# Quadrant matmuls, column-tiled kv and longer DMA runs in a fused attention and MoE kernel

## The chip, the cores and the metric

One core of one Trainium2 chip. The metric is device time in microseconds (us) from the first to the last instruction's completion, as the runs report it; lower is better. A profiled execution also has a span, which is about 1.7 us shorter than the reported time of the same run. The TensorE clock that was granted is given as a share of full speed.

## The reference, cut to what matters

```python
# q, k, v: (8 batches, 8 heads, 576 tokens, 64); w_in (512, 2048), w_out (2048, 512), beta (2048)
q_s = softmax(q, axis=-1)                       # over the 64 features of a head
k_s = softmax(k, axis=2)                        # over the 576 tokens
kv  = einsum('bhsd,bhse->bhde', k_s, v)         # 64 x 64 per head
x   = einsum('bhsd,bhde->bhse', q_s, kv)        # -> (4608 tokens, 512)
h   = x @ w_in
g   = h * sigmoid(beta * h)
out = g @ w_out
```

All inputs and outputs are float32; the kernel multiplies in bfloat16.

## The kernel before

The kernel works on nine chunks of 512 tokens: the first 512 tokens of each batch, and one chunk that holds the last 64 tokens of all eight batches. A chunk has 16 units. A unit is four h matmuls (512 columns each), a tanh on ScalarE and a multiply on VectorE that makes g. Four acc matmuls (g times w_out, 512 columns) of an older chunk are put between two units. The attention of the next batch is slipped in between: exponentials, sums, the kv matmuls (k_s times v) and the x matmuls (q_s times kv).

Two heads share the 128 rows. So kv of a pair of heads is a 128x128 product of which only two 64x64 blocks are wanted, and x uses a block-diagonal matrix `kvp` whose other half is zeros:

```python
    def kv_mm(b, j, n="K"):
        ...
        for t in range(K5):                       # 5 token groups
            nc.tensor.matmul(
                kvs[b, j // 2][:, j % 2, :],                                    # 128 x 130
                Ek[b][:, t, 2 * j : 2 * j + 2, :].rearrange("p h d -> p (h d)"),
                va[b % 2][:, t, j, :],
                start=(t == 0), stop=(t == K5 - 1),
            )

    def x_mm(b, j, n=None):
        ...
        nc.tensor.matmul(
            xps[b, j][:], kvp[b][:, j, :], qT[b][:, :, j, :], start=True, stop=True
        )
```

The loads of batches 0 and 1 and of w_in, and the way the first part is ordered:

```python
    def load_q(b, hf):                            # 1 KB runs, all 128 partitions
        ...
        nc.sync.dma_start(
            t,
            q[b, 4 * hf : 4 * hf + 4, 0:CH, :].rearrange("h (p t) d -> p h (t d)", t=NT),
        )
    ...
    load_w_in(0, 256, 0, 2)                       # 256-column blocks: 1 KB runs
    load_w_in(0, 256, 2, 4)
    for n0 in (256, 512, 768):
        load_w_in(n0, n0 + 256)
    ...
    dummy(24)                                     # matmuls on zeros while the loads come
    q_exp(0, 0, 4)
    q_exp(0, 4, 8)
    q_sum(0, 0, 4)
    q_div(0, 0, NT, nc.gpsimd, 0, 4)              # the two divisions on two engines
    q_sum(0, 4, 8)
    k_exp(0, 0, 4)
    q_div(0, 0, NT, nc.vector, 4, 8)
    ...
```

The softmax here doesn't subtract the row's maximum and nothing guards it: scores larger than these inputs give would overflow.

## Time and profile before

| | before |
|---|---|
| time, median of 3 runs | 287.14 us (286.96 to 287.19) |
| first h matmul starts | 14.40 us |
| first acc matmul (batch 0's h is done) | 30.09 us |
| last of batch 0's values v has landed | 12.98 us |
| last of batch 1's values v has landed | 46.05 us |
| span | 285.5 us |

From the page of the kernel before: the busy time of the engines, the TensorE row of the 40 slices (a digit is tenths busy), the shares of the chain that ended last, and two groups of instructions (line, engine, operation, shapes, count; busy us and mean ns of one; idle time before them and what ended it). PE is TensorE's matmuls, PEld its weight loads, DVE VectorE, ACT ScalarE, POOL GpSimd; SPq is the queue of SyncE, which issues most DMAs.

```profile
span 285.5 us, 4276 instructions
PE 279.2 (98%) x1490; PEld 133.3 (47%) x1490; DVE 157.8 (55%) x303; ACT 169.5 (59%) x275; POOL 79.4 (28%) x135
PE   8998999999999999999999999999999999999995
PE 82%; DMA 14%; POOL 1%; SPq 1%; issue 0%; ACT 0%; POOLq 0%; ACTq 0%
...
L415 PE MATMUL h<-xT,w_in_b 128*128 128x512 bf16 x512 | 129.6, 379 | 1.2 <-DVE g L429 0.6
L415 PEld LDWEIGHTS <-w_in_b 128*128 128x128 bf16 x576 | 56.1, 98 | 69.2 <-POOL w_in_b L154 2.9
```

TensorE is busy 98% and is 82% of the chain. A matmul's 379 ns is its whole passage; what counts for time is the distance between starts, and the timeline of TensorE shows it. Here is the steady state before (start, busy us of the group, what, count):

```profile
114.78 0.73 PE L283 MATMUL kv<-va,Ek 128*128 128x130 bf16 x10
115.35 1.03 PE L467 MATMUL acc<-w_out_b,g 128*128 128x512 bf16 x4
116.21 1.03 PE L415 MATMUL h<-xT,w_in_b 128*128 128x512 bf16 x4
117.07 0.38 PE L360 MATMUL x<-qT,kvp 128*128 128x512 bf16 x1
117.29 1.03 PE L467 MATMUL acc<-w_out_b,g 128*128 128x512 bf16 x4
```

Four acc take 116.21 - 115.35 = 0.86 us, so 216 ns each. Ten kv matmuls take 115.35 - 114.78 = 0.57 us, so 57 ns each, and a batch has 20: 1.14 us. One x takes 0.22 us, and a batch has four: 0.86 us.

The start is bound differently. These are the stretches view (from and to in us, length; busy time of PE, PEld, DVE, ACT and POOL, each with its count of instructions; granted TensorE clock; DMA share; GB/s) and, below it, the DMA view of the first 16 us in 40 slices of 0.4 us, before:

```profile
0.00:8.00 8.00, 6.75 (x18) 2.49 (x19) 3.41 (x10) 3.60 (x4) 5.81 (x23) 1.00 0.79 245
8.00:16.00 8.00, 7.73 (x80) 4.51 (x78) 5.96 (x16) 6.16 (x10) 5.01 (x9) 1.00 1.08 355
16.00:32.00 16.00, 14.86 (x68) 6.24 (x67) 10.92 (x16) 10.88 (x16) 12.05 (x16) 1.00 1.05 381
44.00:56.00 12.00, 11.71 (x75) 6.05 (x73) 9.98 (x24) 11.28 (x20) 4.66 (x6) 1.00 1.07 364
```
```profile
GB/s 0 0 0 0 18 74 205 369 381 369 384 376 356 313 312 338 369 313 349 374 350 378 353 364 374 359 352 360 356 366 349 351 348 341 341 353 356 346 351 351
```

DMA is full from 2.8 us on, at about 355 GB/s. TensorE's clock shows no half-speed stretch behind the dummies. The view counts time before the first clock record (7.20 us here) as 1.00. TensorE is idle for 1.1 us between 16 and 32 us.

### The profile page before, as it was taken

The page shows a single profiled execution, that of the slowest core. Times are in us where ns is not written, and L with a number is a line of the kernel's source. Part 1 is how long each engine was busy: PE and PEld are TensorE (multiplying, and loading weights), DVE is VectorE, ACT ScalarE, POOL GpSimd, SP SyncE. Part 2 cuts the span into 40 slices and gives each one's busy share as a digit, 9 for nine tenths or more (in the row PEclk, how much of TensorE's full clock was granted, in tenths as well). Part 3 has the DMA queues.
Part 4 walks back from the last instruction along what each step waited for, and adds up shares of the span by engine and source line. Part 5 has one row for each costly group of instructions (what it writes and reads, how often), then busy time and mean ns, then how long its engine had stood idle before and what let it go on. Part 6 is the DMA issues. An engine that isn't in the chain of part 4 may idle for free.

```text
span 285.5 us, 4276 instructions
## 1 busy us (share of the span) xinstructions
PE 279.2 (98%) x1490; PEld 133.3 (47%) x1490; DVE 157.8 (55%) x303; ACT 169.5 (59%) x275; POOL 79.4 (28%) x135
## 2 busy tenths in 40 slices
PE   8998999999999999999999999999999999999995
PEld 2543445454454444444454445444544444444444
DVE  3856347976866485647564766466553433334401
ACT  4776258957964587358845884568453544454411
POOL 7667954540631054104510261017000000000000
PEclk9999999999999999999999999999999999999999
DMA  7999999989499917990699059913300111031112
GB/s 232 356 365 386 381 354 353 363 211 363 102 217 360 179 38 174 356 226 36 135 322 282 20 129 238 350 39 78 110 37 0 73 39 38 0 75 39 37 73 74
DMA packets 55782, 51.67 MB, mean 181 GB/s; under 512 B 21184, under 2 KB 48208, under 8 KB 55760
## 3 DMA queue, kind: packets, MB, share of 16 engines
q1 hardware_dynamic: 55584, 51.33, 61.2%
q8 instruction: 11, 0.18, 0.3%
q14 instruction: 11, 0.09, 0.1%
q10 hardware_dynamic: 176, 0.07, 0.1%
HBM read 38.28 MB, written 9.44 MB: 167 GB/s over the span
## 4 chain that ended last, share of the span: by engine, by line
PE 82%; DMA 14%; POOL 1%; SPq 1%; issue 0%; ACT 0%; POOLq 0%; ACTq 0%
PE acc L467 39%; PE h L415 39%; DMA wo<-in_moe_w_out_dram 4%; DMA q<-in_q_dram 4%; PE kv L283 2%; DMA k<-in_k_dram 2%; DMA v<-in_v_dram 2%; DMA wi<-in_moe_w_in_dram 2%; PE x L360 2%; SPq L124 0%; PE xt L385 0%; POOL va L154 0%; SPq L122 0%; PE kv L310 0%; ACT xT L145 0%
## 5 line engine op out<-in xcount | busy, mean ns | idle before, releaser
L429 DVE SCALAR_TENSOR_TENSOR g<-th,h 128x512 bf16<-128x512 bf16 x144 | 98.3, 686 | 96.8 <-ACT th L427 96.6
L427 ACT ACTIVATE th<-h,beta_h 128x512 bf16<-128x512 f32 x144 | 98.4, 688 | 88.6 <-PE h L415 88.4
L467 PE MATMUL acc<-w_out_b,g 128*128 128x512 bf16 (+2 forms) x608 | 145.0, 368 | 0.0
L415 PE MATMUL h<-xT,w_in_b 128*128 128x512 bf16 x512 | 129.6, 379 | 1.2 <-DVE g L429 0.6
L415 PEld LDWEIGHTS <-w_in_b 128*128 128x128 bf16 x576 | 56.1, 98 | 69.2 <-POOL w_in_b L154 2.9
L467 PEld LDWEIGHTS <-g 128*128 128x128 bf16 x608 | 57.2, 98 | 61.9 <-issue 0.4
L194 POOL TENSOR_TENSOR Eq<-Eq,qz 128x512 bf16<-128x512 bf16 (+1 forms) x26 | 30.6, 1179 | 89.8 <-issue 41.8
L190 DVE TENSOR_REDUCE qz<-Eq 128x8 f32<-128x512 bf16 (+1 forms) x27 | 21.0, 778 | 8.9 <-ACT Eq L182 8.9
L182 ACT ACTIVATE Eq<-q 128x512 bf16<-128x512 f32 (+1 forms) x26 | 18.9, 728 | 10.5 <-DMA q<-in_q_dram 10.5
L496 ACT ACTIVATE o<-acc 128x512 f32<-128x512 f32 x34 | 20.0, 591 | 7.4 <-PE acc L467 7.0
L252 ACT ACTIVATE Ek<-k 128x640 bf16<-128x640 f32 (+1 forms) x30 | 22.9, 769 | 1.3 <-DMA k<-in_k_dram 0.9
L154 POOL TENSOR_SCALAR_AFFINE_SELECT va<-v 128x256 bf16<-128x256 f32 (+1 forms) x55 | 21.0, 420 | 2.9 <-DMA v<-in_v_dram 2.9
L415 PE MATMUL h<-xTt,w_in_b 128*128 128x512 bf16 x64 | 16.4, 379 | 0.0
L360 PE MATMUL x<-qT,kvp 128*128 128x512 bf16 x30 | 11.2, 379 | 0.2
L145 ACT CAST xT<-x 128x512 bf16<-128x512 f32 (+1 forms) x19 | 10.6, 559 | 0.7 <-PE x L360 0.6
L154 POOL TENSOR_SCALAR_AFFINE_SELECT w_in_b<-wi 128x512 bf16<-128x512 f32 (+2 forms) x16 | 9.5, 614 | 3.8 <-DMA wi<-in_moe_w_in_dram 3.8
L553 PE MATMUL warm<-zero 128*128 128x512 bf16 x27 | 9.2, 509 | 1.2 <-DVE zero L516 1.2
L236 POOL TENSOR_TENSOR Et<-Et,zt 128x512 bf16<-128x512 bf16 x4 | 4.2, 1042 | 21.9 <-DVE zt L235 21.9
L159 DVE CAST xT<-x 128x512 bf16<-128x512 f32 (+1 forms) x15 | 9.7, 649 | 0.7 <-PE x L371 0.7
L283 PEld LDWEIGHTS <-Ek 128*128 128x128 bf16 x120 | 7.8, 97 | 2.8
L283 PE MATMUL kv<-va,Ek 128*128 128x130 bf16 x120 | 8.8, 220 | 0.0
L154 POOL TENSOR_SCALAR_AFFINE_SELECT w_out_b<-wo 128x1024 bf16<-128x1024 f32 x8 | 8.3, 1039 | 1.5 <-DMA wo<-in_moe_w_out_dram 1.4
(55 smaller groups left out, 76.8 us busy)
## 6 DMA issues: line engine op xcount, KB each, us to landing
k<-in_k_dram SPq DMA_DIRECT2D x28, 320.0 KB, 7.0
v<-in_v_dram SPq DMA_DIRECT2D x26, 320.0 KB, 7.5
q<-in_q_dram SPq DMA_DIRECT2D x16, 512.0 KB, 5.9
out_dram<-o SPq DMA_DIRECT2D x31, 256.0 KB, 3.8
wo<-in_moe_w_out_dram SPq DMA_DIRECT2D x8, 512.0 KB, 11.1
wi<-in_moe_w_in_dram SPq DMA_DIRECT2D x7, 512.0 KB, 9.2
out_dram<-o SPq DMA_DIRECT2D x9, 128.0 KB, 2.3
k<-in_k_dram SPq DMA_DIRECT2D x4, 256.0 KB, 6.8
```

What stands on the lines that cost most here:

```text
L154: nc.gpsimd.affine_select(out=dst, in_=src, pattern=[[0, n]], base=0, channel_multiplier=0, compare_op=ALU.is_equal, fill=fill0,)
L182: nc.scalar.activation(Eq[b][:, :, h0:h1, :].rearrange("p t h d -> p h t d"), ld["q", b, hf][:, a : a + h1 - h0, :].rearrange("p h (t d) - ...
L190: nc.vector.tensor_reduce(qz[b][:, :, h], Eq[b][:, :, h, :], axis=AX.X, op=ALU.add)
L194: eng.tensor_tensor(Eq[b][:, t0:t1, h0:h1], Eq[b][:, t0:t1, h0:h1], qz[b][:, t0:t1, h0:h1].unsqueeze(3).to_broadcast((P, t1 - t0, h1 - h0, ...
L252: nc.scalar.activation(Ek[b][:, :, h0:h1, :].rearrange("p t h d -> p h t d"), ld["k", b, hf][:, a : a + h1 - h0, :].rearrange("p h (t d) - ...
L283: nc.tensor.matmul(kvs[b, j // 2][:, j % 2, :], Ek[b][:, t, 2 * j : 2 * j + 2, :].rearrange("p h d -> p (h d)"), va[b % 2][:, t, j, :], st ...
L360: nc.tensor.matmul(xps[b, j][:], kvp[b][:, j, :], qT[b][:, :, j, :], start=True, stop=True)
L415: nc.tensor.matmul(hs[n, i][:], w_in_b[:, kt, i * P : (i + 1) * P], rhs_a(n, kt), start=(kt == 0), stop=(kt == KT - 1),)
L427: nc.scalar.activation(th[:], h[:], ACTF.Tanh, scale=beta_h[:, i : i + 1])
L429: nc.vector.scalar_tensor_tensor(out=g[:], in0=th[:], scalar=1.0, in1=h[:], op0=ALU.add, op1=ALU.mult)
L467: nc.tensor.matmul(acc[n, st][:, c0:c1], gs[n, j][:, min(st, 3) * P : (min(st, 3) + 1) * P], w_out_b[:, j, c0:c1], start=(j == 0), stop=(j ...
L496: nc.scalar.activation(o[:], acc[n, st][:], ACTF.Copy, scale=0.5)
```

## The change

Its intent: do the attention products without the wasted blocks, and read memory in longer runs.

- x runs in 64x64 quadrants of the array: four small products at once on the four quarters, in all batches. The zero blocks, the mask and `kvp` go.
- kv of batches 2 to 7 runs in column tiles: 40 matmuls of 65 columns, two heads side by side.
- Batches 0 and 1 are read in 2 KB (q) and 2.3 KB (k, v) runs and use row tiles (64 rows) for kv. Their order of work is rewritten.
- w_in is read in 512-column blocks (2 KB runs); a unit takes every fourth column of a block, and four units advance together in halves of K. w_out is read in 4 KB runs.
- The 24 dummies become 5 float32 ones.

The diff, cut to its core:

```diff
+    def early_q(b):
+        for g in range(2):
+            for a in range(2):
+                rows = q[b, 4 * g + a : 4 * g + 4 : 2, 0:CH, :]
+                nc.sync.dma_start(
+                    early("q", b, g, QT8)[a:P:2],                 # every second partition
+                    rows.rearrange("c (r t) d -> r c (t d)", t=QT8),   # 2 KB runs
+                )
+    def early_kv(which, src, b, g):
+        for c in range(2):
+            h = 4 * g + 2 * c
+            nc.sync.dma_start(
+                early(which, b, g, KT9)[:, c],
+                src[b, h : h + 2].rearrange("a (r t) d -> (a r) (t d)", t=KT9),
+            )
...
+    def kv_group(b):
+        ...
+                for c in range(2):
+                    h = 4 * (j // 2) + 2 * c + j % 2
+                    nc.tensor.matmul(
+                        ps[c * D : (c + 1) * D, j, 0 : D + 1],
+                        Ek[b][:, t, h, :],
+                        vt(b)[:, t, h // 2, (h % 2) * VH : (h % 2) * VH + D + 1],
...
+    def x_group(b, gs, names):
+        ...
+            for c, a, r, o, j in quads(g):       # r: 64 rows, o: 64 columns
+                nc.tensor.matmul(
+                    xps[b, 2 * g + c][o, :], kvn[b][r, j, :], ...
...
-                w_in_b[:, kt, i * P : (i + 1) * P],
+                w_in_b[:, kt, blk * CH + r : (blk + 1) * CH : 4],
...
-    dummy(24)
...
-    q_div(0, 0, NT, nc.gpsimd, 0, 4)
...
+    dummy(5, CH)
+    eq_exp(0, 0)
+    eq_exp(0, 1)
...
+    eq_sum(0, 0)
+    eq_div(0, 0, nc.vector)
+    eq_sum(0, 1)
+    eq_div(0, 1, nc.vector)
+    ev_cast(0, 0, 1, nc.gpsimd)
+    eq_t(0, 0, "X0", nc.scalar)
     dummy(1)
+    ekv_open(0, 0, ("X1", "K"))
+    ekv_mm(0, 0)
...
```

## The prediction

> **What bounds the kernel now.** TensorE. The page has PE busy 279.2 of 285.5 us; the chain of waits is 82% PE, mostly the 512-column groups h and acc. Starts of successive matmuls in the timeline: every 216 ns at 512 columns, 57 ns at 130, 29 ns at 64. So h and acc are about 249 us that the change does not touch. Per batch the rest is 4 x-matmuls (0.86 us), 20 kv matmuls (1.14 us), and small ones.
> Two phases are not at that bound. (a) The first h matmul starts at 14.4 us, behind batch 0's loads. (b) After it I count 3.1 us of gaps beyond the normal spacing: 1.6 us at 16.1 to 23.6 us (waiting for cast w_in), 0.9 us at 43.4 to 46.3 us (batch 1, whose last v lands at 46.0 us), 0.3 us at 68 us, 0.2 us at 212 us. Until 46 us DMA is saturated (slices show 9): 350 to 360 GB/s with 1 and 1.25 KB packets, 388 GB/s with 2 KB packets.
>
> **What changes.**
> 1. Longer runs for q, k, v of batches 0 and 1 and for w_in: at 388 GB/s I estimate batch 0's last v at 11.9 us instead of 13.0, the end of w_out at 33.4 instead of 36.4, batch 1's last v at 42.2 instead of 46.0. But both q divisions of batch 0 now sit on VectorE: exp (1.06), sum (1.22), reciprocal (0.25) and division (1.64) put the first h matmul at about 13.6 us, and batch 0's second half interrupts it. Four units per w_in block, in K halves, let the casts (0.59 us each) keep ahead. I expect batch 0's h phase to end near 28.4 us (before: 30.1), and batch 1's gaps to shrink: -2.5 to -3 us, all critical, as PE is gapless afterwards.
> 2. x in quadrants: two rounds of 216 ns a batch instead of four, -0.43 us. Against it: the Trainium skill ("TensorEngine Tiling (Array Packing)", Key Properties) says a change of tiling mode drains TensorE. The only row-tiled matmul here (bt, 16 rows) shows about 0.1 us more than normal spacing on each side. So -0.2 us a batch.
> 3. kv in column tiles: 40 matmuls of 65 columns a batch instead of 20 of 130. Ideal: half of 1.14 us. But the same page (Restrictions) says column tiling disables the fast weight load, and there are twice as many loads. Estimate 0.7 to 1.3 us plus two mode changes: -0.2 to +0.4 us a batch, six batches.
> 4. Tail tokens: 64 small matmuls instead of 32 at 29 ns: +0.3 us in all. Mask, memsets, half the norm work go: off the critical path (VectorE 55% busy). W_in columns at stride 4 may slow weight loads, hidden under 216 ns. W_out in 4 KB runs: no PE effect.
>
> Sum: -2.7 (start) -1.5 (x) +0.3 (kv) +0.3 (tail): about -4 us.
>
> **Predicted: 283.0 us**, 8 in 10 between 279.0 and 287.0. Faster by over 2%: 0.27; within 2%: 0.70; slower: 0.03.
>
> **What would show it.** First acc matmul near 28.4 us; batch 1's v landing near 42 us; DMA near 388 GB/s early; under 1.3 us of PE gaps from there to 50 us; x taking 0.6 to 0.7 us of PE time a batch and kv 0.9 to 1.5 us, mode changes included (distance between the surrounding 512-column matmuls); h and acc still 216 ns apart.
>
> **What would make it wrong.** Nearly free mode changes and quadrants that truly overlap (-8 us, near 279); column-tile weight loads that serialise (+1 us a batch, 288); a stride-4 weight load over 216 ns (tens of us); a stall at batch 0's longer VectorE chain.

## The result, and the profile after

The time is 288.94 us, median of 4 runs (288.32 to 288.96), against 287.16 us (286.96 to 287.25) before in the same rounds. A ratio here is the mean time of one kernel's fast runs over the mean of the other's of the same rounds, so not quite the ratio of the medians quoted: 1.0058, with a 95% interval of 1.0040 to 1.0075. The change is within 2%, and it makes the kernel slower, by about 1.7 us, where the prediction had 4 us in the other direction.

The same lines of the page after:

```profile
span 286.6 us, 4698 instructions
PE 277.5 (97%) x1710; PEld 137.1 (48%) x1710; DVE 154.6 (54%) x283; ACT 168.3 (59%) x280; POOL 73.3 (26%) x119
PE   7599999999999999999999999999999999999995
PE 91%; DMA 2%; ACT 2%; SPq 1%; DVE 1%; POOL 1%; issue 0%; ACTq 0%
...
L475 PE MATMUL h<-xT,w_in_b 128*128 128x512 bf16 x512 | 129.4, 380 | 0.6 <-ACT xT L166 0.6
L475 PEld LDWEIGHTS <-w_in_b 128*128 128x128 bf16 x576 | 64.8, 113 | 61.4 <-issue 1.5
```

TensorE is less busy than before (277.5 against 279.2 us) and still the kernel ends later, so it waits more: the second slice of its row falls from 9 to 5. Weight loads of w_in at stride 4 take 113 ns instead of 98, which stays hidden under 216 ns.

Steady state after, timeline of TensorE:

```profile
114.52 1.03 PE L475 MATMUL h<-xT,w_in_b 128*128 128x512 bf16 x4
115.47 0.82 PE L402 MATMUL kv<-va,Ek 128*64 128x65 bf16 x40
116.23 1.04 PE L527 MATMUL acc<-w_out_b,g 128*128 128x512 bf16 x4
117.10 1.03 PE L475 MATMUL h<-xT,w_in_b 128*128 128x512 bf16 x4
118.06 0.63 PE L426 MATMUL x<-qT,kvn 64*64 64x512 bf16 x8
118.62 1.04 PE L527 MATMUL acc<-w_out_b,g 128*128 128x512 bf16 x4
```

The last of the four h before kv starts at 114.52 + 3 x 0.216 = 115.17, and the first acc after kv at 116.23: 1.06 us, less the h's own 0.216, is 0.85 us for kv (before 1.14). For x it is 118.62 - 117.75 - 0.216 = 0.65 us (before 0.86). The steady state gains, as intended. The start does not, in the stretches view and the first 16 us of DMA after:

```profile
0.00:8.00 8.00, 6.48 (x8) 2.76 (x9) 2.66 (x5) 2.54 (x3) 1.51 (x12) 1.00 0.69 205
8.00:16.00 8.00, 4.98 (x67) 3.53 (x65) 4.90 (x12) 5.98 (x10) 3.38 (x5) 0.91 0.99 367
16.00:32.00 16.00, 16.00 (x91) 8.19 (x88) 10.40 (x20) 10.16 (x18) 11.74 (x19) 0.94 1.03 393
44.00:56.00 12.00, 11.10 (x113) 5.75 (x110) 7.43 (x20) 7.73 (x17) 3.37 (x5) 1.00 1.05 352
```
```profile
GB/s 0 0 0 0 0 31 113 220 384 384 307 358 251 307 245 303 321 387 264 222 288 357 409 401 403 421 392 426 392 415 354 374 392 378 385 379 394 287 220 282
```

Three things are to be seen. The DMA rate swings between 220 and 390 GB/s until 8 us and only then goes to 400. TensorE is busy for only 4.98 of 8 us from 8 to 16 us. And its clock falls to a mean of 0.91 and 0.94: the trace's record of the clock has it at half speed from 14.56 us for 3.41 us. The chain that ended last (start, us, what; pieces of under 0.1 us left out) says what TensorE waits for there:

```profile
5.20 6.13 DMA v<-in_v_dram
11.38 1.46 POOL va L175
12.89 0.69 PE kv L274 x18
```

It is v of the first half, issued behind the loads of q and k, and its cast on GpSimd. This load of v was issued at 5.20 us and landed at 11.32; the same half of v had landed by 9.65 before.

To place the loss, the start of each chunk's last tanh shows how far a kernel has come (16 tanh a chunk; times from the traces, in brackets the difference from before):

| stage | before | after | quadrants and column tiles alone (first experiment) |
|---|---|---|---|
| first h matmul | 14.40 | 17.22 (+2.81) | 15.38 (+0.97) |
| first acc matmul | 30.09 | 31.98 (+1.88) | 29.95 (-0.14) |
| tanh 16 (end of batch 0) | 30.29 | 32.61 (+2.31) | 30.15 (-0.14) |
| tanh 32 (end of batch 1) | 67.61 | 71.67 (+4.06) | 67.80 (+0.20) |
| tanh 112 | 214.82 | 215.87 (+1.05) | 212.11 (-2.71) |
| tanh 144 (last) | 270.07 | 271.12 (+1.05) | 267.36 (-2.71) |

So after loses 2.3 us by the end of batch 0's tanh (1.9 us of it ahead of the first acc), another 1.75 us by the end of batch 1 (4.06 - 2.31), wins 3.0 us between tanh 32 and 112, and is level from there. Of the 3.0 us, five batches at 0.50 us (0.29 from kv and 0.21 from x) are 2.5 us; the tail tokens give 0.2 us (their matmuls take 0.94 us of TensorE's time instead of 1.13), and two waits at 68 us of before, 0.33 us together, are gone. The +0.97 us of the first experiment at the first h comes with a half-clock stretch of its profiled run, from 11.56 us for 3.41 us, although it has the 24 dummies; by its first acc nothing of it is left.

The chain of waits shows what happens in batch 1's stretch (start, us, what; pieces of under 0.1 us left out), after:

```profile
46.45 0.31 ACT kvn L297
...
47.11 1.26 ACT Ek L246 x2
48.39 0.59 ACT xT L166
49.03 1.24 PE h L475 x5
```

and before:

```profile
39.43 5.79 DMA v<-in_v_dram
45.37 0.87 POOL va L154 x2
46.28 0.44 PE kv L310 x5
```

Before, this stretch hangs on a load of v, which landed at 45.22 us. After, k's second half has landed at about 44.2 us (estimated from the loads beside it, 43.45 and 44.96 us), but its exponential (`Ek`, 1.26 us) stands in ScalarE's queue behind the scaling of the first half's kv (`kvn`), and the output of x (`xT`) behind that.

### The profile page after: what moved, and what is told of

It reads as the page before. It is cut to its first block, busy times and chain, and to the rows that moved or that the text cites. A ratio compares the mean times of both kernels' runs of the same rounds, so it can differ in the third digit from the quotient of the medians.

```text
span 286.6 us, 4698 instructions
## 1 busy us (share of the span) xinstructions
PE 277.5 (97%) x1710; PEld 137.1 (48%) x1710; DVE 154.6 (54%) x283; ACT 168.3 (59%) x280; POOL 73.3 (26%) x119
## 4 chain that ended last, share of the span: by engine, by line
PE 91%; DMA 2%; ACT 2%; SPq 1%; DVE 1%; POOL 1%; issue 0%; ACTq 0%
PE acc L527 43%; PE h L475 43%; DMA v<-in_v_dram 2%; PE x L426 2%; PE kv L402 2%; PE kv L274 1%; SPq L111 1%; DVE g L489 1%; POOL va L175 1%; SPq L119 1%; ACT th L487 0%; ACT Ek L246 0%; PE tp L233 0%; ACT xT L166 0%; PE xt L440 0%
## 5 line engine op out<-in xcount | busy, mean ns | idle before, releaser
L475 PEld LDWEIGHTS <-w_in_b 128*128 128x128 bf16 x576 | 64.8, 113 | 61.4 <-issue 1.5
L333 POOL TENSOR_TENSOR Eq<-Eq,qz 128x512 bf16<-128x512 bf16 x24 | 25.1, 1050 | 87.5 <-issue 41.1
L175 POOL TENSOR_SCALAR_AFFINE_SELECT va<-v 128x256 bf16<-128x256 f32 (+2 forms) x53 | 21.1, 434 | 9.3 <-DMA v<-in_v_dram 9.2
L373 ACT ACTIVATE Ek<-k 128x640 bf16<-128x640 f32 x24 | 17.5, 730 | 0.0
L331 DVE TENSOR_REDUCE qz<-Eq 128x8 f32<-128x512 bf16 x24 | 16.2, 677 | 0.5 <-ACT Eq L323 0.5
L323 ACT ACTIVATE Eq<-q 128x512 bf16<-128x512 f32 x24 | 14.9, 624 | 0.0
L180 DVE CAST xT<-x 128x512 bf16<-128x512 f32 x16 | 10.9, 684 | 0.8 <-PE x L426 0.8
L166 ACT CAST xT<-x 128x512 bf16<-128x512 f32 x16 | 9.3, 579 | 2.7 <-PE x L426 2.6
L175 POOL TENSOR_SCALAR_AFFINE_SELECT w_in_b<-wi 128x512 bf16<-128x512 f32 x16 | 9.5, 612 | 3.8 <-DMA wi<-in_moe_w_in_dram 3.7
L603 PE MATMUL warm<-zf 128*128 128x512 f32 (+1 forms) x14 | 8.6, 762 | 1.5 <-DVE zf L571 1.5
```

Of the source, the lines that this page charges most:

```text
L166: nc.scalar.copy(dst, src)
L175: nc.gpsimd.affine_select(out=dst, in_=src, pattern=[[0, n]], base=0, channel_multiplier=0, compare_op=ALU.is_equal, fill=fill0,)
L180: eng.tensor_copy(dst, src)
L323: nc.scalar.activation(by_pair(Eq[b], m).rearrange("p t h d -> p h t d"), ld["q", b, hf][:, a : a + 2, :].rearrange("p h (t d) -> p h t d" ...
L331: nc.vector.tensor_reduce(z, e, axis=AX.X, op=ALU.add)
L333: nc.gpsimd.tensor_tensor(e, e, z.unsqueeze(3).to_broadcast((P, NT, 2, D)), ALU.mult)
```

## The experiments

Rival theories after reading the traces: (T1) quadrants and column tiles cost more than they show, through mode changes; (T2) the new weight layout costs; (T3) the start of batch 0 costs, through slow loads, through the halved clock, or through its longer chain; (T4) batch 1's order of work costs. Medians are given with the median of before in the same rounds.

### Parts of the change alone

**Quadrants and column tiles alone** (for batches 2 to 7 and the tail tokens; batches 0 and 1 and the weights as before):

```diff
 # before.py plus
+    kvn, kv_group, x_group, xt_group       # as in the changed kernel, for b >= 2
```

> The kernel before, with only the steady-state part of the change: batches 2 to 7 take kv in column tiles and x in 64x64 quadrants, the tail tokens of batches 2 to 7 in quadrants; batches 0 and 1, w_in, w_out and all loads stay as before. Theory (the quadrants gain, the start loses): from the traces of before and after, the 256th h matmul to the 448th is 3.0 us nearer together, so I expect 284.1 us, 0.5 us on either side, ratio 0.989. Rival (the mode changes eat the gain, and the lost time is there): 287 us or more. PE time from the last h matmul before a group to the next acc matmul: kv about 1.07 us, x about 0.87 us, each with one 0.22 us h matmul in it.

Measured 284.52 us against 287.05, ratio 0.9906 (0.9890 to 0.9923). T1 falls: this part alone gives 2.9 of the 3.0 us from tanh 32 on, and this is the fastest kernel; it beats both. From tanh 112 on it stands 2.71 us ahead of before (the table above). The loss is in the other parts.

**The weight layout alone** (w_in in 512-column blocks, w_out in 4 KB runs, all else as before):

```diff
-                w_in_b[:, kt, i * P : (i + 1) * P],
+                w_in_b[:, kt, blk * CH + r : (blk + 1) * CH : 4],
```

> The kernel before, with only the weights' part of the change: w_in in 512-column blocks with columns taken at stride 4, four h units per block in halves of K, w_out in 4 KB runs, beta as four rows. Loads of batches 0 and 1 and all attention work as before. Theory: this part is sound; the 1.6 us of gaps that wait for cast w_in go, w_out lands 1 to 2 us earlier at over 400 GB/s, batch 1's data too; the first h matmul waits some 0.5 us more for w_in. I expect 286.0 us (285.0 to 287.0). Rival: the weights' layout is part of the loss (stride-4 weight loads, the later first block, the bunched units that keep ScalarE waiting): 287.5 us or more.

Measured 287.53 us against 287.05, ratio 1.0011 (0.9996 to 1.0025). A miss: no gain, as its rival said. Its first acc comes at 30.88 us, 0.79 us later than before; of that 0.2 us stays at the end. TensorE sits idle longer for cast w_in than before (three waits, 1.6 us together, against two, 0.5 us together), so the four units in K halves do not keep ahead of the casts here. **The reverse, after with the old weight layout:**

```diff
-                w_in_b[:, kt, blk * CH + r : (blk + 1) * CH : 4],
+                w_in_b[:, kt, i * P : (i + 1) * P],
```

> The kernel after, with w_in, w_out and beta loaded, cast and used as before (256- and 512-column blocks, 2 KB w_out runs, contiguous weight columns, units one by one). Theory: the weights' part is nearly neutral in the kernel before (run e2: +0.4 us), so also here: 288.0 to 289.0 us. Rival: the four-unit blocks carry the early loads' gain, and without them it is 290 us or more; or they are the loss, and it is below 287.5 us.

Measured 288.55 us against 287.20, ratio 1.0042 (1.0009 to 1.0076): taking the layout away mends nothing that is clear of noise. T2 is worth at most some tenths.

**The first experiment's kernel with the new batch 1, and with the new batch 0** (the diffs in short, not in code):

```diff
-    kvp, load_q, load_kv, kv_pair for b == 1       # old way
+    early_q, early_kv, ekv_mm, x_group for b == 1  # new way
```

> Run e1 (before plus quadrants for batches 2 to 7) with batch 1 alone loaded and computed as in after (2.3 KB runs, row tiles, quadrants, five h units held open until the last quarter of K). Theory: from the 16th to the 32nd tanh after loses 1.75 us against before, and it loses the same in e3 whose start is 0.8 us earlier, so it is batch 1's own order of work: 286.3 us, 1.8 us more than e1. Rival: that loss follows from the late start of batch 0, then 284.5 us as e1.

Measured 286.60 us against 287.20, ratio 0.9971 (0.9935 to 1.0008): 2.1 us more than the first experiment's kernel.

```diff
-    kvp, load_q, load_kv, kv_pair for b == 0
+    early_q, early_kv, ekv_mm, x_group for b == 0
```

> Run e1 with batch 0 alone loaded and computed as in after (2 KB and 2.3 KB runs, row tiles, quadrants, f32 warm-up), weights and batch 1 as before. Theory: batch 0's part costs what the first acc matmul shows in after, about 1.9 us, with the same slow packets at 5 to 9 us and a window of half clock: 286.5 us (286.0 to 287.3). The parts then add up: e1 284.5, batch 0 +2, batch 1 +1.8, weights +0.4, together 288.7 against 288.9 measured for after. Rival: batch 0's part gains by its shorter loads, 284 us or less, and the loss lies in how the parts meet.

Measured 286.44 us against 287.20, ratio 0.9968 (0.9936 to 0.9999): 1.9 us more. The sum closes: 284.5 + 2.1 + 1.9 + 0.4 (weights) = 288.9, and after is 288.94. By the ratios, which use the before of the same rounds, the sum is 0.9906 + 0.0065 + 0.0062 + 0.0011 = 1.0044 against 1.0058; the 0.4 us between them lie within the intervals. T3 and T4 hold, and the two are nearly equal.

### Batch 1: the order of work

**The exponential of k's second half ahead of the scaling of kv** (after, two lines moved):

```diff
+        for c in range(2):
+            ek_exp(1, 1, c)
         ekv_rk(1, 0, D)
         ekv_norm(1, 0, nc.vector, nc.scalar)
-        for c in range(2):
-            ek_exp(1, 1, c)
```

> The kernel after, with the two exponentials of k of batch 1's second half issued on ScalarE before the scaling of the first half's kv instead of behind it; nothing else. In the trace of after they wait from 43.5 us (k landed) to 47.1 us behind that scaling, and the second half's x comes 7 us after its v. Theory (ScalarE's order in batch 1 is part of the 2 us lost between the 65th and the 128th h matmul): 0.7 to 1.2 us less than after, 288.0 us. Rival (that loss is the bunched units' tanh queue and the waits for batch 1's loads): less than 0.3 us.

Measured 288.34 us against 287.05, ratio 1.0034 (1.0011 to 1.0058). The stage from tanh 16 to 32 loses 1.27 us instead of 1.75: 0.48 us are back, between the theory's 0.7 to 1.2 and the rival's 0.3.

**The same, and the third quarter of K of five units not taken ahead of their tanh:**

```diff
-        for i in range(5):
-            unit_mm(1, i, 2, 3)
...
-            unit_a(n, i, ... 3 if n == 1 and i < 5 else 0)
+            unit_a(n, i, ... 2 if n == 1 and i < 5 else 0)
```

> The kernel after, with two changes of order in batch 1: the exponentials of the second half's k ahead of the first half's kv scaling (as e4), and the third quarter of K of the five open h units taken unit by unit with the fourth instead of for all five first. Theory (batch 1's loss of 1.75 us between the 16th and the 32nd tanh is ScalarE and VectorE starting late on bunched units): the loss falls to 0.7 us or less, 1.0 us or more less than after: 287.9 us or less. Rival: the bunching does not matter, then as e4, 288.3 us.

Measured 287.83 us against 287.41, ratio 1.0008 (0.9987 to 1.0029). The time is as expected; the stage loses 0.86 us, where 0.7 or less was expected. Half of batch 1's loss was the order in which queues were filled, at no other cost: 0.48 us in ScalarE's and 0.41 us by the order of the quarters of K.

### Batch 0: loads or clock

**Three more dummies, so that TensorE is not idle** before batch 0's kv (after):

```diff
     dummy(1)
+    dummy(3, CH)
     ekv_open(0, 0, ("X1", "K"))
```

> The kernel after, with three more 512-column f32 warm-up matmuls on zeros between the first transposes and the first kv matmuls, where TensorE was idle from 9.9 to 12.9 us; nothing else. Theory: that idle time drops the granted clock to half for one or two windows of 3.4 us (clock record 0.5 from 14.6 to 18.0 us in the profiled run, mean clock 0.988 in the other runs), which costs half of the matmul time in them. I expect the clock record to show no 0.5 after the start, a mean granted clock near 1.00, and 287.0 us (286.5 to 287.8), that is 1 to 2 us less than after. Rival: the start waits for loads and casts, not for TensorE, so the clock does not matter: 288.5 to 289 us.

Measured 287.36 us against 287.05, ratio 1.0016 (0.9993 to 1.0040); the mean clock is 1.0 in all four runs, and 1.6 us of the time are back (1.2 us by the ratios). In its profile first h comes at 16.35 and first acc at 31.22. The time gains more than the 0.75 us of first acc because after's profiled run is its luckiest (288.32 us, mean clock 0.994; the other three have 0.988, about twice as long at half speed, and take 288.92 to 288.96 us). The next two fences are TensorE's timeline in after (in brackets the idle time and what ended it) and with the dummies:

```profile
12.89 0.69 PE L274 MATMUL kv<-va,Ek 64*128 64x130 bf16 x18 [3.02 <-POOL va L175]
...
16.13 1.15 PE L274 MATMUL kv<-va,Ek 64*128 64x130 bf16 x18
17.22 0.96 PE L475 MATMUL h<-xT,w_in_b 128*128 128x512 bf16 x2
```
```profile
15.67 0.69 PE L274 MATMUL kv<-va,Ek 64*128 64x130 bf16 x18
16.35 0.59 PE L475 MATMUL h<-xT,w_in_b 128*128 128x512 bf16 x2
```

The same 18 kv matmuls of the second half take 1.15 us at half clock and 0.69 us at full. Here the Trainium skill ("TensorE: Matmul & The Clock Gate", Part 1, What's actually happening) agrees with the trace in the length of the window: it says that the clock falls to half after about one idle window of 3.4 us, and the clock records have stretches of 3.41 and 6.83 us. The idle times were shorter: 3.02 us in after, ahead of the first kv, and 1.41 us in the first experiment's profiled run. In all 13 profiled runs that have such a stretch it begins 6.83 us after the clock came up, which happened between 4.42 and 7.74 us. What decides whether it comes is not shown: the run told next has 2.14 us of idle time and no such stretch. That the added dummies keep it away is well seen: in all 44 runs of after and its ten variants without them the mean clock is 0.994 or less, in all 16 runs of the four kernels with them 0.998 or more.

**Together with the mended batch 1:**

```diff
+    dummy(3, CH)          # and the batch-1 order of the run before
```

> The kernel after with the warm-up of e3 and the batch 1 order of e11 together; nothing else. Theory: the two losses are separate, so the gains add: 288.9 less 1.6 less 1.1, 286.2 us (285.7 to 286.8), faster than before by 0.3% but behind e1 with 284.5 us. Rival: both gains are the same late chain seen twice: 287.2 us.

Measured 287.43 us (286.70 to 288.36) against 287.41, ratio 1.0002 (0.9977 to 1.0027). A miss: the profiled run, 286.70, has both gains, but the other three are slower. Something in the start still varied, and it was not the clock (0.999 to 1.0 in all four).

**What makes the first loads slow.** In after, 17 of some 900 packets of the first 9 us took 0.5 to 1.5 us where a 2 KB packet otherwise takes 84 ns (before had 6 over 0.5 us, the longest 0.66), and batch 0's last v landed at 14.31 us (before 12.98). Four guesses, one after the other; the first three all missed.

```diff
-                    early("q", b, g, QT8)[a:P:2],              # every second partition
+                    early("q", b, g, QT8)[a * KR : (a + 1) * KR],   # 64 in a row
```

> The kernel after, with q of batches 0 and 1 loaded to partitions 0 to 63 and 64 to 127 instead of to every second partition (the x matmuls take the matching columns); nothing else. In after and two variants of it some packets of the first 2 KB and 2.3 KB loads take 0.5 to 1.6 us instead of 0.08, between 5 and 9 us, and batch 0's data lands 1.3 us later than before. Theory (the every-second-partition q loads do that): the slow packets go, batch 0's last v lands near 12.3 us instead of 14.3, and the time is 1 to 2 us less, near 287.3 us. Rival (it comes with the first large packets whatever their place): still slow, last v near 14 us, 288.3 to 289 us.

Measured 290.42 us against 287.20, ratio 1.0106 (1.0076 to 1.0135): worse, and slow also where batch 1's q is loaded.

```diff
-    early_kv("k", k, 0, 0)
+    for g in range(2):
+        early_kv("k", k, 0, g, nc.scalar)         # k's loads issued by ScalarE
```

> The kernel after, with the four k loads of batch 0 issued by ScalarE's queue at the start, beside q on SyncE; nothing else. In after SyncE needs 0.6 to 0.8 us to issue each 256 KB q load, about as long as its data takes, so the queue stays shallow in the first 3 us. Theory (the slow start of the loads is this issue rate): from 2 to 8 us the rate rises from 270 to 350 GB/s or more, batch 0's last v lands at 12.5 to 13 us instead of 14.3, and the time is about 1 us less, 288 us. Rival (the packets themselves are slow there): last v still at 14 us or later, packets of 1 us and more still in the list, 288.5 to 289.5 us.

Measured 289.89 us against 287.41, ratio 1.0072 (1.0043 to 1.0101). The rate stayed low (209 GB/s from 4 to 6 us).

```diff
+                for c in range(2):                # each q load in two, 128 KB each
+                    nc.sync.dma_start(
+                        early("q", b, g, QT8)[a:P:2, c], ...
```

> The kernel after, with q of batches 0 and 1 in eight loads of one head each (64 rows of 2 KB, a contiguous 128 KB of memory) instead of four of two heads; nothing else. Theory (a load that steps over two heads per partition is slow to issue and lets the DMA engines fall out of step): issue falls from 0.62 to about 0.35 us each, the slow packets get fewer, last v near 13 us, 288 us. Rival: slow packets as before, last v at 14 us or later, the time as after or more.

Measured 289.42 us against 287.41, ratio 1.0077 (1.0053 to 1.0101). The packets over 1 us went, but each half load still took 0.60 us to issue, and the last v landed at 15.19 us. So the packets over 1 us are not what makes the loads late.

Four more runs then separated the size of a packet from the set of partitions that a load writes. Three of them read other rows of q into place, so they are wrong. The comparison cannot vouch for q here; q is drawn with a spread of 0.1, its softmax is almost flat.

```diff
 # q of batch 0: 1 KB runs, the same 64 partitions (wrong rows)
+                        early("q", b, g, QT8)[a:P:2].rearrange("p c (m n) -> p (c m) n", n=256),
+                        rows.rearrange("(m r n) -> r m n", m=4, n=256),
```

> After, with batch 0's q read in 1 KB packets instead of 2 KB, into the same 64 partitions, same number of loads and bytes (other rows of q are read, so the result is wrong on purpose). Theory A (packets of 2 KB and more are slow at the start): packets over 0.7 us go from the first 7 us, rate at 2 to 8 us back to about 340 GB/s, last v at 13.3 us or before, time near 287.5. Theory B (loads that write only every second partition are slow): nothing changes, slow packets stay, last v near 14.3, time 288 to 289.

```diff
 # q of batch 0: 1 KB runs over all 128 partitions (wrong rows)
+                        early("q", b, g, QT8)[:, a].rearrange("p (m n) -> p m n", n=256),
+                        q[b, h : h + 2, 0:CH].rearrange("h (p t) d -> p h (t d)", t=4),
```

> After, with batch 0's q in 1 KB packets over all 128 partitions, as many loads and bytes as after (rows land in other places, so the result is wrong on purpose). A and B: slow packets of q go, last v 13.3 us or before, time near 287.5. If k and v in 2.3 KB packets are the slow ones (C): no gain, last v near 14.3.

```diff
 # k and v of batch 0 in 768 B runs
+                    src[b, h : h + 2].rearrange("a (r m t) d -> (a r) m (t d)", t=3, m=3),
```

> After, with batch 0's k and v read in 768 B packets instead of 2304 B, same loads, bytes and partitions (v's casts in three pieces); the result is right. C: packets over 0.7 us go, rate at 4 to 8 us near 340 GB/s, last v at 13.3 us or before. A and B: q's loads stay slow, last v near 14, time 288 to 289.

```diff
 # q over all 128 partitions, and k and v in 768 B runs
```

> After, with both: q in 1 KB packets over all 128 partitions, k and v in 768 B packets (wrong on purpose). Any of A, B, C: no packet over 0.7 us in the first 9 us, 340 GB/s at 2 to 8 us, last v at 13.3 us or before, time 287 to 287.8. If it stays slow, the size and pattern of packets are not the cause, and the order or time of the issues is.

| run | time | before | ratio (95%) | last v lands | first h | first acc |
|---|---|---|---|---|---|---|
| after | 288.94 | 287.16 | 1.0058 (1.0040 to 1.0075) | 14.31 | 17.22 | 31.98 |
| q in 1 KB, 64 partitions | 289.40 | 287.24 | 1.0065 (1.0041 to 1.0088) | 14.29 | 17.54 | 33.18 |
| q in 1 KB, 128 partitions | 288.40 | 287.24 | 1.0035 (1.0014 to 1.0056) | 13.15 | 16.90 | 31.77 |
| k, v in 768 B | 288.69 | 287.24 | 1.0053 (1.0025 to 1.0081) | 14.82 | 16.78 | 32.26 |
| both | 288.15 | 287.24 | 1.0032 (1.0009 to 1.0055) | 13.78 | 16.39 | 31.73 |

The size of q's packets does nothing (14.29). Loads of q over all 128 partitions bring the last v forward by 1.16 us (14.31 to 13.15), and each of these q loads is issued in about 0.47 us instead of 0.61 to 0.77. The last v load is issued 1.19 us earlier (7.92 instead of 9.11) and takes the same 5.2 us to land: the gain is already there when it is issued. The short runs of k and v make it later again. Single packets over 0.5 us remain in every run, so what makes a packet slow is not found; they go neither with size nor with partitions. And the expected times of about 287.5 were not reached by any.

In the profiles, q over 128 partitions moves first acc by only 0.21 us from after. But these two profiled runs differ in the clock, and the run with q in 1 KB over 64 partitions is the fair neighbour: its last v lands as in after, and it is at half speed for 6.83 us, as is the run over 128 partitions. The stretch from 8 to 16 us, first over 64 partitions, then over 128:

```profile
8.00:16.00 8.00, 4.83 (x66) 3.63 (x64) 4.53 (x10) 6.04 (x10) 3.34 (x5) 0.86 1.02 377
8.00:16.00 8.00, 5.21 (x68) 4.22 (x70) 4.80 (x12) 5.20 (x10) 4.32 (x7) 0.71 1.04 389
```

Between these two, first acc comes 1.41 us earlier (31.77 instead of 33.18) and the time is 1.0 us shorter (288.40 instead of 289.40, same rounds). So the loads are worth about a microsecond; after's profiled run hides it, being the one of after's four with the shorter half-clock stretch.

**Both mended at once**, and then with batch 1's order as well:

```diff
 # q of batch 0 over 128 partitions (wrong rows), and
+    dummy(3, CH)
```

> The load of q as in e14 (1 KB packets over 128 partitions, wrong rows on purpose) with the three dummy matmuls of e3. In e14 the last v landed 1.16 us earlier than in after, but the clock was at half speed for 6.83 us (11.38 to 18.21 us) and the first acc moved by only 0.21 us. Theory (the halved clock ate what the loads gave): the clock stays at 1.0, first h near 15.3 us, first acc at 30.1 to 30.5 us (before 30.09), the end near 286.2. Rival (w_in's loads or casts, not the clock, hold the h phase): first acc stays at 31.2 us or later, as in e3.

```diff
 # the same, and the batch-1 order of above
```

> e17 with batch 1's order as in e11. If the three parts (loads, clock, order) are what took the gain away: first acc 30.1 to 30.5 us, a loss of 0.9 us between tanh 16 and 32, the later stages 3.0 us shorter, so about 285.1, ratio near 0.993. If something else is missing from the account: 286.3 or more.

The first measured 286.88 us (286.74 to 286.89) against 287.18, ratio 0.9989 (0.9974 to 1.0004); the second 285.62 us (285.38 to 286.66) against 287.18, ratio 0.9958 (0.9932 to 0.9985). Both ends miss what was expected (286.2 and 285.1), by 0.7 and 0.5 us. The first of them in the stretches view:

```profile
8.00:16.00 8.00, 7.50 (x91) 4.75 (x91) 5.47 (x14) 6.21 (x12) 4.12 (x6) 1.00 1.02 365
```

| stage, difference from before | after | dummies alone | q loads alone | both | both and order |
|---|---|---|---|---|---|
| first h matmul | +2.81 | +1.95 | +2.50 | +0.94 | +0.86 |
| first acc matmul | +1.88 | +1.13 | +1.68 | +0.31 | -0.15 |
| tanh 16 to 32 | +1.75 | +1.75 | +1.74 | +1.74 | +0.86 |
| tanh 32 to 144 | -3.01 | -3.01 | -3.01 | -3.01 | -3.01 |

In these profiles dummies alone give 0.75 us of first acc, loads alone 0.21, both 1.57, as if the two costs hid one another. The times do not bear that out: by the ratios, over all runs, dummies alone give 1.2 us, loads alone 0.7 and both 2.0, so they add. The 0.21 is small because after's profiled run was at half speed for 3.41 us and that of the loads alone for 6.83. With both, the expected first acc (30.1 to 30.5) is met at 30.40. The last kernel is no version to keep, as its q is wrong, and the first experiment is 1.1 us faster than it. And even with all three mended, first acc comes only 0.15 us earlier than before.

What is left of batch 1's loss, 0.86 us, can be read in the chain of the last kernel (pieces of under 0.1 us left out), though no run took it out:

```profile
50.84 0.70 DVE qz L340
51.56 0.20 DVE qz L341
51.76 0.56 DVE qz L340
52.35 0.20 DVE qz L341
52.55 1.15 DVE g L498 x2
```

The sums of batch 2's q (`qz`), which nobody needs yet, stand in VectorE's queue ahead of the first g of batch 1, and TensorE waits for g. The new batch-1 code issues them there. That it is the whole of the 0.86 us is argued, not shown.

## Why the prediction was wrong

Point by point, in its own order.

1. *The start, "-2.5 to -3 us".* This is the step that failed, and the only large one. It took the 388 GB/s that 2 KB packets reach later and put it at the very first loads, so that batch 0's last v would land at 11.9 us; it landed at 14.31, later than before. Loads of q over every second partition are part of it (over all 128, issued faster, 1.16 us came back); what the slow packets cost is not shown. The later loads were priced too low as well: the end of w_out came at 37.03 us where it had 33.4, batch 1's last v at 45.72 where it had 42.2. It had first h at "about 13.6 us", behind the divisions of q on VectorE; it was 17.22, and the path was another: TensorE waited 3.02 us for v of the first half, which had landed at 11.32 us (before 9.65), and for its cast on GpSimd. It had "batch 0's h phase" end at 28.4; it ended at 31.98. The term of -2.7 us measured about +4 us: +2.31 by the end of batch 0 and +1.75 in batch 1 in the stages, +1.9 and +2.1 when each was put alone into the first experiment's kernel.

   Two mechanisms were missing. During the half-clock stretch behind that wait, 3.41 us in the profiled run and about twice as long in the other three, matmuls ran at half speed; the prediction did not look at the clock. That there are 5 dummies instead of 24 is not the likely reason: the 5 float32 ones keep TensorE busy for 7.63 us, nearly as long as the 24 did (8.28). The wait behind them is new, and filling it ended the stretch. And batch 1's loss is not in the landing of its loads: its v landed 0.3 us sooner than before, and still its stage lost 1.75 us, half of it to the order of work in the queues (0.48 us in ScalarE's, 0.41 us in the quarters of K).

   That four units in K halves keep ahead of the casts is not shown either: from first h to first acc it took 15.69 us before and 14.76 after, but after starts 2.8 us later, when more of w_in is cast, and with the layout alone, starting at 14.68, it took 16.20.
2. *x in quadrants, "-0.2 us a batch".* Right: 0.65 us instead of 0.86. The Trainium skill ("TensorEngine Tiling (Array Packing)", Key Properties) says that a change of tiling mode drains the engine; the trace agrees and puts a size on it. The first x starts 309 ns after the last h instead of 216, and acc starts 308 ns after the last round of x instead of 216: 93 ns on each side.
3. *kv in column tiles, "-0.2 to +0.4 us a batch".* The size was off: -0.29. The same page (Restrictions) says column tiling disables the fast weight load, and the prediction had taken that for a cost. The trace has a column-tile matmul of 65 columns starting every 16 ns on average (two start together, about every 30 ns), mode changes of 93 ns in and 112 ns out apart, so no weight load is seen to hold it. With it the sum's +0.3 us for six batches would have been -1.7.
4. *Tail tokens and the rest.* Small, but with the other sign: 0.94 us for the 64 matmuls, mode changes included, against 1.13 for the 32 before, -0.2 us where it had +0.3. h and acc stayed at 216 ns, and stride 4 slowed a weight load from 98 to 113 ns, hidden. The last stages of after have the same length as before.

Of the listed risks none is what happened. The last, "a stall at batch 0's longer VectorE chain", is not seen: with loads and clock mended first h is still 0.94 us late, but VectorE sat idle for 1.58 us ahead of it, waiting for the first kv. That kv started at 11.90 us, right behind the added dummies, with v's cast done at 11.56. The steady state was underrated (-3.0 us measured, -0.9 in the sum's x and kv and tail terms), and the start outweighed it.

## What to carry to other kernels

A part that shortens steady work and a part that rewrites the start are two changes; time each alone, since here the first was worth 2.5 us and the second took 4 us away. Do not price the first loads of a kernel at the rate that later loads of the same packet size reach, nor let a wait open behind the dummy matmuls without asking whether the matmuls after it will run at half clock. When mending one cost at the start moves a profile by little, see first whether the two profiled runs had the same granted clock: here a gain of about 1 us looked like 0.21.

## What the Trainium skill lacked or had wrong

- "TensorEngine Tiling (Array Packing)": Key Properties has the drain at a change of mode but no figure. Here it cost 93 ns on each side of 64x64 tiles, and 93 ns in and 112 ns out for 128x64 column tiles. Restrictions does not say what the loss of the fast weight load costs: the column-tile matmuls of 65 columns started 16 ns apart on average, so nothing that the trace shows.
- "TensorE: Matmul & The Clock Gate", Part 1, agrees on the window (stretches of 3.41 and 6.83 us at half speed), but idle times shorter than the window it names came before a half-clock stretch (3.02 us, and 1.41 us in the first experiment's profiled run), while 2.14 us in another run did not bring one. Between executions of one kernel the stretch can differ by a whole window: mean clock 0.994 in one run of after, 0.988 in three, which took 0.6 us longer.
- "DMA: Bandwidth & Descriptors", Rules for kernel authors, advises one transfer over 128 partitions instead of two over disjoint halves. The runs agree (last v at 13.15 us with q over 128 partitions, 14.31 us with every second one in each load; 290.42 us with 64 in a row); the page has no figure for it.
- No page describes single packets of 0.5 to 1.5 us among a kernel's first loads (first 9 us here), beside 84 ns for a usual 2 KB packet. Their cause is open: neither packets of 768 B nor other partitions did away with them.
